# Down weights through two streams of buffers, and a new written order, in a one-core kernel of a long convolution with a routed FFN

## Chip, core and metric

One core of a Trainium2 chip. The metric is device microseconds of one launch, the median of three runs. A profiled execution is one more run, with the hardware profiler on; "span" is the time from its first to its last instruction.

## The reference

Inputs are q, k, v of 2048 x 512, float32. Cut to what matters:

```python
k_shift = sum over t in 0..3 of k_pad[:, t:t+S] * shift_k[:, 3-t]     # 4 taps, causal, per channel
kv = k_shift * v
y  = causal convolution of kv with ssm_k, 2048 long, per channel (by FFT) + kv * ssm_D
a  = q * y
r  = q @ w_r;  idx = the two tokens with the largest r
f  = (silu(x_sel @ w_gate) * (x_sel @ w_up)) @ w_down * sigmoid(r_sel)   # for these two tokens only
b  = q + f scattered to the two tokens
g  = sigmoid(q . gate_w)
out = g * a + (1 - g) * b
```

w_gate and w_up are 512 x 1792, w_down is 1792 x 512.

## The kernel before

The 512 channels are worked in four blocks c = 0..3 of 128. The long convolution is a transform of 2048 points, cut in two short stages with a 32 x 32 transpose between, done for kv and for the filter, a product, and the way back. For a block the steps are, with the name that they have in the written order:

- `D t` (L138): POOL adds the skip weight into the filter tile hN; one for each of the eight hN tiles, t = 2c and 2c + 1.
- `A c.b` (L152): first stage of the filter, two matmuls from hN, then a DVE transpose into tile e (L150).
- `taps c.x` (L163): the four taps. ScalarE scales (L168, L175), POOL adds (L177); in two of the sixteen groups DVE does both (L172).
- `T c.x` (L179): 16 TensorE transposes of the taps' result, then two DVE products with vN (L192).
- `C c.b` (L197): first stage of kv, as A.
- `S c.u` (L208): second stage, 16 matmuls; ScalarE copies one half (L222), DVE multiplies (L229), and every second S has two sums over tile y (L237) on POOL (on DVE for S3.6 and S3.7).
- `I c.u` (L240): back, first stage, 16 matmuls into two PSUM tiles, each emptied by ScalarE (L259) or DVE (L261) into tile f. I3.1's second one is emptied by DVE.
- `X c.i` (L263): DVE transpose of half of f (L268).
- `J c.m` (L289): back, second stage. For c < 3: 8 matmuls, ScalarE applies the gate (L317), POOL multiplies by qN (L320), SP stores (L323). For c = 3: 16 matmuls, a DVE product (L310), a sum on POOL, or on DVE for J3.3 (L312), and the store. `Q 3.m` (L281) prepares q for the last block on ScalarE, `Y x` (L271) loads it.

The routed FFN is one generator, of which each `G` in the order takes one step, 43 in all: G1 to G8 the router scores (one qT tile each, L353), G9 the gates, G10 to G14 the two largest scores by four TensorE transposes (L340) with DVE and POOL steps between, G15 the token numbers and the gather of their rows (L386, an indirect DMA from POOL), G16 and G17 the gathered rows (L401, L408), G18 to G25 the gate weights and G26 to G33 the up weights (one tile each, L425), G34 the transpose of the product, G35 to G42 the down weights (L443; wd0 to wd7 below, wd0 and wd1 being the two halves of the first row block), G43 the sum over blocks (L452) and the scaling (L454). `Z0` (L457) adds the two rows into the output by an indirect DMA; it follows every store and G43.

Loads: each stream (L73) is a list of DMAs into a ring of tiles. `Lh` loads the filter tiles hN (2 buffers), `Lk` the taps' input kT (2), `Lv` vN (3), `Lq` qN (4), and `Lw` the stream wff (2): 8 qT tiles, 8 gate, 8 up and 8 down tiles, 32 loads. `L0` to `L10` load constants, w2 (the second stage's matrix) in two halves `L4` and `L5`, vv (J's matrix) by `L10`. All loads and stores are issued by SP, in order; a load waits until its buffer's last reader is done, and whatever is behind it on SP waits too.

What sets the order is the text ORDER (L33): a list of 533 names. At each name the step's generator is advanced by one piece, and what it emits goes to the end of the queue of its engine:

```python
    with tc.manual_schedule():
        for name in ORDER.split():
            next(work[name], None)
```

So every engine works strictly in the order of this text. PSUM holds three tiles "p2" for A, T, C, S, I and J3, one "ps" for the other J, one "pf" for the FFN.

Of the kernel before, what the change touches and what calls it, by code (L numbers as in the profile page):

```python
# [594 lines left out]
```

## Time and profile before

| what | value |
|---|---|
| median of 3 runs | 169.28 us (167.88, 169.28, 171.59) |
| the profiled execution | 167.47 us, span 165.7 us |
| busy: TensorE, VectorE, ScalarE, GpSimd | 132.6, 117.1, 105.7, 116.3 us |
| mean granted TensorE clock | 0.943 |
| moved by DMA | 39.8 MB |

How to read the lines below: engines are PE (TensorE matmuls), PEld (its weight loads), DVE (VectorE), ACT (ScalarE), POOL (GpSimd), SP (SyncE; SPq is its queue). A timeline row is: start us, length us, engine, line, operation, output and inputs, count, and in brackets how long the engine had been idle before and what ended that. One float32 matmul of the source is two MATMUL records, so an S is x32, a J of c < 3 x16, a down step x8. In a row of groups stand the busy time, the mean ns of one, and the idle time ahead of them.

### The profile page before, as it was taken

What the parts mean: (1) busy time and instruction counts of PE and PEld (TensorE: products, weight loads), DVE (VectorE), ACT (ScalarE), POOL (GpSimd) and SP (SyncE); (2) the same over time, 40 slices, a digit from 0 to 9 for tenths busy, and PEclk for the clock granted to TensorE, in tenths of its full rate; (3) what the DMA queues carried; (4) which work ended last, traced back from release to release, by engine and by line L of the source; (5) the groups of instructions that cost most, each with busy time, mean ns of one, the idle gap of its engine ahead of it and who ended that gap; (6) DMA issues with size and microseconds to landing.
All of it is one profiled execution on the core that took longest, in us unless ns stands there. A gap on an engine that the chain in (4) does not pass through costs nothing.

```text
span 165.7 us, 5116 instructions
## 1 busy us (share of the span) xinstructions
PE 132.6 (80%) x2156; PEld 64.0 (39%) x2156; DVE 117.1 (71%) x120; ACT 105.7 (64%) x201; POOL 116.3 (70%) x109
## 2 busy tenths in 40 slices
PE   0079699898859889489999999999999898696270
PEld 0033245442313333263446545355445454274040
DVE  0649899999654796644999769999929987673400
ACT  4537578847756457324679959865499888966010
POOL 0079899999776996824999999558936974077303
PEclk9999999999996999965999999999999999999955
DMA  5999999979993008903685671907778877898820
GB/s 175 303 381 352 333 403 398 377 267 337 408 362 102 0 6 357 365 13 120 252 277 192 235 285 20 321 19 248 230 243 266 279 267 200 237 299 276 304 104 1
DMA packets 16420, 39.82 MB, mean 240 GB/s; under 512 B 2123, under 2 KB 2828, under 8 KB 16270
## 3 DMA queue, kind: packets, MB, share of 16 engines
q1 hardware_dynamic: 16334, 39.50, 68.4%
q8 instruction: 17, 0.28, 0.6%
q0 software_dynamic: 64, 0.01, 0.1%
q14 instruction: 5, 0.04, 0.1%
HBM read 35.30 MB, written 4.20 MB: 238 GB/s over the span
## 4 chain that ended last, share of the span: by engine, by line
PE 42%; DMA 36%; DVE 9%; ACT 4%; SPq 3%; issue 3%; POOL 1%; POOLq 1%; DVEq 0%
DMA wff<-in_wd_dram 10%; PE p L217 9%; DMA vN<-in_vN_dram 9%; PE p L204 7%; PE p L159 7%; PE p L251 5%; PE pf L425 4%; PE ps L304 4%; DMA wff<-in_qT_dram 4%; DMA wff<-in_wu_dram 4%; DVE e L150 4%; DMA pe<-in_qrow_dram,ti 3%; DMA out_dram<-e 3%; ACT f L259 3%; DMA w<-in_w_dram 3%; DVE y L229 3%
## 5 line engine op out<-in xcount | busy, mean ns | idle before, releaser
L177 POOL TENSOR_TENSOR acc<-acc,tap 128x512 f32<-128x512 f32 x42 | 53.6, 1284 | 7.0 <-ACT tap L175 5.7
L229 DVE TENSOR_TENSOR y<-p,g 128x1024 f32<-128x1024 f32 x32 | 38.0, 1214 | 13.7 <-ACT g L222 12.8
L150 DVE STREAM_TRANSPOSE e<-p 128x1024 f32<-128x1024 f32 x32 | 38.2, 1230 | 7.6 <-PE p L204 3.2
L237 POOL TENSOR_TENSOR y<-y 128x512 f32<-128x512 f32 x30 | 38.1, 1288 | 5.2 <-DVE fac L412 3.3
L175 ACT ACTIVATE tap<-kT,shk 128x512 f32<-128x512 f32 x42 | 29.7, 723 | 10.7 <-POOL acc L177 10.4
L217 PE MATMUL p<-e,w 64*32 64x256 f32 x1024 | 34.8, 393 | 1.2 <-DVE kv L192 0.6
L159 PE MATMUL p<-hN,w 64*128 64x512 f32 x64 | 20.3, 724 | 10.7 <-DMA w<-in_w_dram 9.4
L222 ACT ACTIVATE g<-p 128x512 f32<-128x512 f32 x32 | 18.8, 599 | 13.6 <-PE p L217 13.0
L217 PEld LDWEIGHTS p<-e,w 64*32 64x32 f32 x1024 | 16.7, 107 | 20.4 <-ACT f L259 3.5
L320 POOL TENSOR_TENSOR qN<-acc,qN 128x512 f32<-128x512 f32 x12 | 15.4, 1288 | 11.9 <-DMA qN<-in_qN_dram 11.3
L317 ACT ACTIVATE acc<-ps,omg,gcol 128x128 f32<-128x128 f32 x48 | 18.1, 461 | 6.6 <-PE ps L304 6.4
L204 PE MATMUL p<-kv,w 64*128 64x512 f32 x64 | 16.6, 640 | 3.3 <-ACT f L259 2.0
L259 ACT ACTIVATE f<-p 128x1024 f32<-128x1024 f32 x15 | 16.3, 1115 | 4.7 <-PE p L251 4.7
L268 DVE STREAM_TRANSPOSE f<-f 128x2048 f32<-128x2048 f32 x8 | 18.1, 2298 | 0.1
L251 PE MATMUL p<-y,w 32*64 32x512 f32 x256 | 16.9, 601 | 0.3 <-DVE e L150 0.3
L168 ACT ACTIVATE acc<-kT,shk 128x512 f32<-128x512 f32 x16 | 11.4, 720 | 4.7 <-DMA kT<-in_kT_dram 3.1
L304 PE MATMUL ps<-f,vv 128*64 128x128 f32 x192 | 13.3, 278 | 0.3 <-ACT acc L317 0.3
L304 PEld LDWEIGHTS ps<-f,vv 128*64 128x64 f32 x192 | 10.3, 134 | 5.9 <-issue 2.7
L159 PEld LDWEIGHTS p<-hN,w 64*128 64x128 f32 x64 | 5.9, 209 | 16.3 <-POOL hN L141 9.8
L192 DVE TENSOR_TENSOR kv<-p,vN 128x512 f32<-128x512 f32 x16 | 10.5, 686 | 1.3 <-DMA vN<-in_vN_dram 1.0
L443 PE MATMUL pf<-wff,pe 112*32 112x256 f32 x64 | 5.6, 422 | 6.8 <-DMA wff<-in_wd_dram 6.7
L204 PEld LDWEIGHTS p<-kv,w 64*128 64x128 f32 x64 | 6.1, 192 | 11.2 <-issue 7.6
(72 smaller groups left out, 99.6 us busy)
## 6 DMA issues: line engine op xcount, KB each, us to landing
vN<-in_vN_dram SPq DMA_DIRECT2D x16, 256.0 KB, 6.4
hN<-in_hN_dram SPq DMA_DIRECT2D x8, 512.0 KB, 5.6
wff<-in_qT_dram SPq DMA_DIRECT2D x8, 512.0 KB, 6.0
wff<-in_wg_dram SPq DMA_DIRECT2D x8, 448.0 KB, 3.7
wff<-in_wu_dram SPq DMA_DIRECT2D x8, 448.0 KB, 4.6
wff<-in_wd_dram SPq DMA_DIRECT2D x8, 448.0 KB, 5.3
qN<-in_qN_dram SPq DMA_DIRECT2D x12, 256.0 KB, 5.8
out_dram<-qN SPq DMA_DIRECT2D x12, 256.0 KB, 3.6
```

Of the source, the lines that this page charges most:

```text
L150: nc.vector.transpose(ee[c][:, i, b * 16:(b + 1) * 16].rearrange("p d k e -> p d e k"), p)
L159: nc.tensor.matmul(p[:, j], w1[r], hs.get(t)[r, 16 * (b % 2):16 * (b % 2) + 16], start=True, stop=True)
L175: nc.scalar.activation(s, w[j], AF.Copy, scale=shk[:, c, j:j + 1])
L177: nc.gpsimd.tensor_add(acc, acc, s)
L204: nc.tensor.matmul(p[:, par].rearrange("p (d e) m -> p d e m", e=2), w1[r], x[r], start=True, stop=True)
L217: nc.tensor.matmul(p[32 * j:32 * j + 32, b, ri].rearrange("p i d -> p (i d)"), w2[r, 4 * u + j, 32 * ri:32 * ri + 32], e[r, :, u + 8 * j, ...
L222: nc.scalar.activation(g, p[:, :, :, 0], AF.Copy)
L229: nc.vector.tensor_mul(y[:, u % 2], p[:, :, :, 1].unsqueeze(3).to_broadcast(shape), g.unsqueeze(2).to_broadcast(shape))
L237: eng.tensor_tensor(w[:, :, 0, n], w[:, :, 0, n], w[:, :, 1, 1 - n], op=op)
L251: nc.tensor.matmul(pp[kp // 2][64 * h:64 * h + 64, kp % 2], w3[r, n], y[(h - kp) % 2][r, :, 0, n], start=(n == 0), stop=(n == 1), skip_gro ...
L259: nc.scalar.activation(to, src, AF.Copy)
L304: nc.tensor.matmul(p[64 * par:64 * par + 64, w * i:w * i + w], vv[:, par * 16 + m0 + i, :], ff[c][:, d, par * 16 + m0 + i, :], start=(i == ...
```

## The change

The four second halves of the down weights (wd1, wd3, wd5, wd7) are no longer loaded by the stream wff but as tiles 8 to 11 of the filter stream hN, whose two buffers the filter's first stage uses until A3.3. wff has 28 loads instead of 32. The array of down weights is laid out as 32 x 32 blocks in its last two dimensions to fit the tile; the bytes and their order are the same, each load is 448 KB as before. With the two wff buffers, four down loads can be under way. The text ORDER is new throughout; it holds the same names, with 12 Lh and 28 Lw instead of 8 and 32.

```diff
--- before.py
+++ after.py
@@ -31,28 +31,28 @@
 
 
 ORDER = """
-Lk L0 taps0.0 taps0.0 Lk Lk Lv L3 Lh L7 L2 Lv L1 Lh Lk Lw Lw taps0.2 taps0.0 taps0.2 taps0.0 taps0.2 taps0.1 D0
-taps0.1 taps0.1 taps0.1 A0.1 A0.1 A0.0 T0.0 D1 A0.3 taps0.2 T0.0 T0.0 Lk Lh Lv Lk Lv taps0.3 taps0.3 taps0.3 taps0.3
-taps1.0 D2 taps1.0 taps1.0 taps1.1 taps1.0 taps1.1 taps1.1 A0.3 A0.0 G A0.2 A0.2 G T0.1 T0.1 T0.1 A1.1 Lk A1.1 Lw Lk
-Lw Lv L4 L5 Lv C0.0 C0.0 C0.1 C0.1 C0.2 C0.2 C0.3 C0.3 taps1.1 taps1.3 taps1.3 taps1.2 G G A1.0 A1.0 T1.0 T1.0 T1.0
-S0.3 S0.3 taps1.3 S0.3 S0.4 S0.4 taps1.2 taps1.3 S0.4 Lw S0.2 S0.2 S0.2 taps1.2 S0.0 S0.0 G Lv S0.0 Lw Lh Lv Lk
-taps1.2 S0.5 S0.5 S0.5 G T1.1 S0.1 S0.1 T1.1 T1.1 S0.1 taps2.0 D3 S0.3 S0.3 S0.5 taps2.0 S0.1 Lw Lk Lw L6 A1.2 C1.0
-A1.2 taps2.1 C1.0 A1.3 A1.3 G G L9 C1.2 G C1.2 C1.1 C1.1 G taps2.1 S0.1 S0.6 S0.6 taps2.0 G I0.0 Lk Lh Lq L10
-taps2.1 Lk Lv taps2.0 S0.6 G Lh D5 C1.3 C1.3 Lv taps2.1 G Lq I0.0 taps2.3 Lv Lk A2.3 S0.7 I0.0 taps2.3 A2.3 D4 S0.7
-S0.7 S1.2 S1.2 S1.2 S0.5 A2.1 A2.1 taps2.3 taps2.3 S1.3 S1.3 S1.3 T2.0 A2.2 S0.7 T2.0 T2.0 G A2.0 A2.0 A2.2 S0.7
-taps2.2 taps2.2 taps2.2 G I0.1 I0.1 I0.1 Lh S1.0 taps2.2 S1.5 S1.5 S1.5 S1.1 S1.0 S1.0 G S1.1 S1.1 Lw Lk T2.1 G Lv
-Lh G S1.4 S1.4 T2.1 T2.1 Lq Lw G Lv Lw Lw S1.4 Lk Lv C2.1 C2.1 C2.0 C2.0 C2.2 C2.2 C2.3 C2.3 G S1.3 X0.1 X0.0
-taps3.1 S1.3 S1.1 S1.1 G I1.0 taps3.1 Lw Lw taps3.1 taps3.1 taps3.0 taps3.0 S1.5 I1.0 I1.0 taps3.0 S1.5 taps3.0 S1.7
-S1.7 S1.7 D7 S1.6 S1.6 S1.6 S2.2 Lk D6 taps3.2 G G J0.3 J0.3 Lv taps3.2 S2.2 Lw Lw T3.0 S1.7 S1.7 T3.0 T3.0 taps3.2
-taps3.2 Lq A3.3 A3.3 J0.2 S2.2 J0.3 J0.2 J0.2 S2.3 S2.3 S2.3 G G I1.1 I1.1 S2.0 S2.0 S2.3 S2.0 S2.1 S2.1 J0.1 I1.1
-S2.1 A3.2 J0.1 Lv A3.2 Lw S2.3 Lw A3.1 taps3.3 J0.3 G G S2.1 A3.1 J0.0 Lw S2.1 X1.1 I2.0 taps3.3 J0.0 X1.0 I2.0 A3.0
-A3.0 I2.0 S2.7 S2.7 S2.7 taps3.3 G S2.6 S2.6 S2.6 S2.5 S2.5 S2.5 J0.2 Lq taps3.3 J0.1 Lw S2.4 S2.4 T3.1 T3.1 Y1 T3.1
-S2.4 S2.7 J1.0 J1.0 G S2.7 C3.0 C3.0 J1.0 Lw S2.5 S2.5 Lq J1.0 Lw Q3.2 C3.1 C3.1 C3.3 C3.3 C3.2 C3.2 J1.2 J1.2 I2.1
-I2.1 I2.1 S3.3 S3.3 S3.2 G G S3.3 S3.2 S3.2 Lq Q3.3 S3.1 S3.1 S3.0 S3.0 Q3.3 J0.0 J0.0 S3.1 S3.0 S3.5 S3.5 S3.5 Y0
-J1.1 Lw Lw X2.1 S3.4 J1.1 J0.1 J1.2 J1.2 S3.4 Q3.2 G G S3.4 J1.3 J1.3 Lq S3.3 S3.3 S3.1 S3.1 I3.0 I3.0 G Lw X2.0
-S3.6 S3.6 S3.6 S3.7 S3.7 S3.7 J2.1 J2.1 Lq G J1.1 J1.1 Lw G J1.3 J1.3 S3.5 S3.5 L8 S3.7 S3.7 I3.0 Lq Lw Lw J2.3 J2.3
-I3.1 I3.1 J2.2 G I3.1 Lq Lq J2.2 Q3.0 G J2.0 J2.0 J2.1 J2.1 Lw Lw J2.2 X3.0 J2.3 J2.0 Q3.1 Q3.0 J2.3 X3.1 J2.2 Q3.1
-J3.0 J3.1 G G J3.2 J3.1 J3.1 J3.3 J3.0 J3.0 J3.2 J3.2 J3.3 J3.3 J2.0 Lw Lw G G J3.1 G J3.0 J3.2 J3.3 Z0
+Lk L0 taps0.0 taps0.0 Lk Lk Lh Lk L2 L3 L7 Lh L1 Lv Lw Lv Lw taps0.1 taps0.0 taps0.1 taps0.0 taps0.2 taps0.2 D0
+taps0.2 taps0.1 taps0.1 A0.0 A0.0 A0.1 T0.0 D1 taps0.2 G taps0.3 taps0.3 taps0.3 T0.0 A0.1 A0.2 A0.2 T0.0 A0.3 A0.3
+G taps0.3 T0.1 Lk Lh Lv Lv Lw Lk Lh Lk Lk Lw L4 Lv taps1.0 D2 taps1.0 taps1.0 taps1.0 taps1.1 taps1.1 D3 taps1.1
+taps1.1 taps1.2 A1.0 T0.1 T0.1 A1.0 C0.2 C0.1 C0.2 C0.1 C0.0 G C0.0 C0.3 C0.3 A1.2 A1.2 A1.1 A1.3 G S0.0 A1.3 A1.1
+taps1.3 taps1.2 S0.0 taps1.3 S0.0 S0.3 T1.0 S0.3 S0.1 taps1.2 taps1.3 S0.1 T1.0 S0.3 Lw Lv L5 Lw Lk Lv taps1.2
+taps1.3 G Lv Lk S0.4 S0.4 T1.0 S0.1 S0.4 taps2.0 G T1.1 T1.1 T1.1 Lw Lw S0.1 S0.1 L6 S0.5 taps2.0 S0.5 S0.5 S0.2
+C1.3 S0.2 S0.2 Lk L9 taps2.1 C1.3 C1.1 C1.1 G G C1.2 C1.2 C1.0 Lk taps2.0 S0.3 S0.3 S0.5 C1.0 S0.5 G I0.0 taps2.0 Lq
+G G S0.6 I0.0 taps2.1 G S0.6 S0.6 taps2.2 S0.7 S0.7 S0.7 taps2.1 Lh D4 I0.0 taps2.2 G A2.1 A2.0 A2.1 G A2.0 S1.3
+S1.3 S1.3 S1.2 S1.2 S1.2 Lh S0.7 S0.7 taps2.2 taps2.1 I0.1 D5 G Lk taps2.3 A2.2 A2.2 I0.1 I0.1 S1.1 S1.1 S1.1 S1.0
+S1.0 S1.0 S1.4 S1.4 S1.4 S1.5 S1.5 Lv T2.0 T2.0 S1.5 taps2.3 taps2.2 G S1.3 S1.3 S1.1 S1.1 taps2.3 Lv Lk G T2.0 S1.6
+I1.0 S1.6 taps3.0 I1.0 L10 taps2.3 Lv Lw Lw taps3.0 I1.0 G G X0.1 X0.0 T2.1 J0.0 Lv T2.1 T2.1 S1.6 A2.3 A2.3 C2.3
+C2.3 C2.2 C2.0 C2.2 C2.1 C2.0 C2.1 taps3.0 taps3.1 S1.7 taps3.0 Lk Lh taps3.1 Lw taps3.1 Lv Lk Lw taps3.3 S1.7
+taps3.1 T3.0 G G J0.0 Lv S1.7 T3.0 S1.5 S1.5 taps3.3 T3.0 S1.7 S1.7 S2.1 S2.1 S2.1 Lv S2.0 S2.0 S2.0 S2.2 J0.3 I1.1
+J0.0 Lw Lw S2.2 Lq J0.0 Lh taps3.3 S2.2 J0.3 Lq J0.1 G taps3.3 I1.1 I1.1 G X1.1 S2.3 J0.1 S2.3 S2.3 S2.5 S2.5 S2.5
+D6 S2.4 S2.4 S2.4 J0.2 A3.1 A3.1 A3.0 S2.1 S2.1 Lw Lw taps3.2 L8 A3.0 J0.1 G S2.3 J0.2 S2.3 X1.0 taps3.2 taps3.2 Lq
+G I2.0 I2.0 D7 S2.6 J0.1 Lv S2.6 S2.6 Lq S2.7 S2.7 Lw Lw S2.7 J0.3 taps3.2 J1.0 S2.7 Y0 I2.0 T3.1 T3.1 S2.5 S2.5
+T3.1 A3.2 A3.2 Y1 J1.0 Q3.3 G J1.0 S2.7 Lh G A3.3 A3.3 C3.1 C3.1 C3.2 C3.0 C3.0 Q3.0 C3.3 C3.3 Q3.1 J1.1 Lw G Lq
+J1.1 I2.1 I2.1 J0.3 J1.0 Lw Lw J0.2 C3.2 S3.1 S3.1 S3.1 J1.1 S3.0 S3.0 I2.1 S3.0 Lq Lq X2.0 S3.1 J1.1 Lh J1.3 J1.3 G
+G Lw Lw S3.3 S3.3 S3.3 S3.2 S3.2 S3.2 Q3.3 S3.4 S3.4 J1.2 S3.4 S3.5 S3.5 S3.5 G X2.1 J1.2 J1.3 S3.1 J1.3 S3.3 J0.2
+Q3.0 S3.3 G S3.6 S3.6 Lw Lw Q3.2 J1.2 I3.0 Lq J1.2 S3.6 J2.3 J2.3 G S3.7 S3.7 S3.7 S3.5 S3.5 Lw Lq G S3.7 S3.7 J2.0
+I3.0 Lq Lq G G I3.1 J2.0 J2.0 I3.0 J2.1 I3.1 I3.1 J2.1 G G J2.2 J2.2 X3.0 J2.3 Lh Lw J2.0 Lw J2.1 Q3.1 J3.0 Q3.2
+J3.1 X3.1 J3.2 Lh J2.3 J2.1 J2.2 J3.0 J3.0 J2.2 J3.0 J3.3 J3.1 J3.1 J3.2 J3.2 J3.1 G G J3.3 J3.3 J3.2 J3.3 G G G Z0
 """
 
 
@@ -94,13 +94,14 @@
                 self.load()
             return self.tiles[k // len(self.cuts)]
 
-    hs = Stream("hN", [128, 32, N2], [a["hN"][t] for t in range(2 * NC)], P["h"])
+
+    hs = Stream("hN", [128, 32, N2], [a["hN"][t] for t in range(2 * NC)] + [a["wd"][fb, :, 1] for fb in range(4)], P["h"])
     kst = Stream("kT", [128, 1216], [a["kT"][c, x] for c in range(NC) for x in range(2)], P["k"], [(0, 704), (704, 1216)])
     vst = Stream("vN", [128, 4, DC], [a["vN"][c, x] for c in range(NC) for x in range(4)], P["v"])
     qst = Stream("qN", [128, 4, 128], [a["qN"][c, m] for c in range(NC - 1) for m in range(4)], P["q"])
     side_src = [a["qT"][c, hf] for c in range(4) for hf in range(2)]
     side_src += [a[nm][hf, kc] for nm in ("wg", "wu") for hf in range(2) for kc in range(4)]
-    side_src += [a["wd"][fb, :, hf] for fb in range(4) for hf in range(2)]
+    side_src += [a["wd"][fb, :, 0].rearrange("p a b -> p (a b)") for fb in range(4)]
     sst = Stream("wff", [128, 1024], side_src, P["wff"])
 
     shk = const.tile([128, NC, 4], F32, name="shk")
@@ -438,7 +439,7 @@
         for fb in range(4):
             for hf in range(2):
                 yield
-                wt = sst.get(24 + 2 * fb + hf)
+                wt = hs.get(8 + fb).rearrange("p a b -> p (a b)") if hf else sst.get(24 + fb)
                 for s4 in range(4):
                     nc.tensor.matmul(pd[32 * s4:32 * s4 + 32, hf * 256:(hf + 1) * 256], hT[:FS, s4, 32 * fb:32 * fb + 32],
                                      wt[:FS, s4 * 256:(s4 + 1) * 256], start=(fb == 0 and hf == 0), stop=(fb == 3),
@@ -569,7 +570,7 @@
     r["wrg"] = wrg
     for n, w in (("wg", B_w_gate), ("wu", B_w_up)):
         r[n] = w.reshape(4, 128, 4, 2, HB).transpose(3, 0, 1, 2, 4).reshape(2, 4, 128, 4 * HB)
-    r["wd"] = B_w_down.reshape(4, 4, FS, 2, 256).transpose(0, 2, 3, 1, 4).reshape(4, FS, 2, 1024)
+    r["wd"] = B_w_down.reshape(4, 4, FS, 2, 256).transpose(0, 2, 3, 1, 4).reshape(4, FS, 2, 32, 32)
     return {n: np.ascontiguousarray(x) for n, x in r.items()}
 
 
```

## Prediction

> **What bounds the kernel now.** I read the chain that ended last from its end backwards, then the timeline of TensorE and its neighbours after 139 us, then the busy time by stretches. The chain's last pieces (start us, us, what):
>
> ```profile
> 20.14 8.93 DMA vN<-in_vN_dram
> ...
> 64.91 5.76 DMA pe<-in_qrow_dram,ti
> ...
> 124.00 6.09 DMA wff<-in_wu_dram
> ...
> 132.63 5.21 DMA wff<-in_wd_dram
> ...
> 138.58 6.59 DMA wff<-in_wd_dram
> ...
> 145.92 4.96 DMA wff<-in_wd_dram
> ...
> 151.56 2.04 PE p L304 x64
> ...
> 154.35 0.93 DVE e L312
> ...
> 155.30 5.60 DMA out_dram<-e
> ```
>
> From 132.6 to 150.9 us the chain is almost nothing but loads of the down weights: four rounds through two wff buffers, each round begun only when TensorE has left the buffer. The timeline of the same stage shows what they hold up:
>
> ```profile
> 139.86 1.97 PE L251 MATMUL p<-y,w 32*64 32x512 f32 x32
> 141.76 1.10 PE L304 MATMUL ps<-f,vv 128*64 128x128 f32 x16
> 141.97 1.24 DVE L261 COPY f<-p 128x1024 f32<-128x1024 f32 x1 [2.21 <-PE p L251]
> 143.31 4.50 DVE L268 STREAM_TRANSPOSE f<-f 128x2048 f32<-128x2048 f32 x2
> 150.92 0.64 PE L443 MATMUL pf<-wff,pe 112*32 112x256 f32 x8 [1.59 <-DMA wff<-in_wd_dram]
> 151.49 2.08 PE L304 MATMUL p<-f,vv 128*64 128x64 f32 x64
> 157.62 1.08 PE L443 MATMUL pf<-wff,pe 112*32 112x256 f32 x8 [0.55 <-DMA wff<-in_wd_dram]
> ...
> 161.34 0.30 ACT L454 ACTIVATE pe<-pf,fac 16x64 f32<-16x64 f32 x1 [1.98 <-PE pf L452]
> 161.93 1.38 POOL L457 DMA_INDIRECT out_dram<-pe,oidx  x1 [7.21 <-ACT pe L454]
> ```
>
> The two X3 transposes are through at 147.81, yet the last two J3 products (L304, x64) start at 151.49, behind the fifth and sixth down weights in TensorE's order. The scatter waits for two branches that end within 0.8 us of each other: the last store (155.30 + 5.60 = 160.90) and the routed tokens' row (161.34 + 0.30 = 161.64). Shortening one alone would bring at most 0.8 us.
>
> The stretches (start:end, length, then busy us of PE, PEld, DVE, ACT, POOL; granted clock, DMA share, GB/s) show the rest:
>
> ```profile
> 40.40:60.70 20.30, 16.73 (x215) 6.42 (x215) 13.14 (x19) 12.45 (x21) 16.64 (x20) 0.92 0.52 200
> 45.60:49.70 4.10, 2.21 (x34) 0.70 (x33) 2.12 (x5) 2.24 (x4) 3.20 (x6) 1.00 0.95 364
> 49.70:53.90 4.20, 4.13 (x25) 1.38 (x33) 1.76 (x4) 2.79 (x5) 2.77 (x6) 0.66 0.33 101
> 66.30:70.40 4.10, 1.89 (x72) 1.07 (x56) 2.75 (x5) 1.59 (x3) 3.58 (x4) 1.00 0.95 367
> 70.40:74.60 4.20, 3.64 (x40) 2.67 (x40) 1.91 (x5) 1.22 (x4) 0.89 (x2) 0.64 0.04 13
> 74.60:78.70 4.10, 4.10 (x48) 1.55 (x46) 1.80 (x2) 1.99 (x4) 2.02 (x3) 0.54 0.36 122
> 80.00:139.80 59.80, 57.58 (x1100) 28.77 (x1096) 52.14 (x44) 47.61 (x95) 47.15 (x40) 1.00 0.66 222
> 143.80:161.00 17.20, 10.09 (x200) 7.20 (x200) 7.70 (x7) 7.44 (x23) 7.62 (x6) 0.88 0.78 262
> ```
>
> From 80 to 139.8 us TensorE is busy 57.6 of 59.8 us: nothing is to be had there by order alone. Before it lie two holes. Around 66 to 70 us TensorE waits for the gathered rows, and its clock then stands at 0.64 and 0.54 for 8.3 us while all others are under half busy. Around 45 to 50 us it waits for the top-2 steps.
>
> **The change, part by part.** The instructions are the same; what changes is where eight loads land and the order. I compared the two ORDER lists name by name, with one unit price for each name from these rows (the L340 rows are tr1 to tr3, the first three of the four transposes in G11 to G14):
>
> ```profile
> 40.45 0.64 PE L353 MATMUL pf<-wff,wrg 128*32 128x256 f32 x8 [0.72 <-DMA wff<-in_qT_dram]
> 45.36 0.30 PE L340 MATMUL pf<-ident,m 128*128 128x128 f32 x1 [0.46 <-DVE m L337]
> 47.49 0.32 PE L340 MATMUL pf<-ident,m 128*128 128x128 f32 x1
> 50.86 0.32 PE L340 MATMUL pf<-ident,m 128*128 128x128 f32 x1
> 59.68 1.13 PE L159 MATMUL p<-hN,w 64*128 64x512 f32 x4 [0.43 <-DVE e L150]
> 70.71 1.17 PE L401 MATMUL pf<-wtrev,pe 2*128 2x32 f32 x8 [2.52 <-DMA pe<-in_qrow_dram,ti]
> 127.89 1.10 PE L217 MATMUL p<-e,w 64*32 64x256 f32 x32
> 130.13 0.59 PE L425 MATMUL pf<-wff,pe 128*32 128x224 f32 x8 [0.62 <-DMA wff<-in_wu_dram]
> 137.88 0.16 PEld L443 LDWEIGHTS pf<-wff,pe 112*32 112x32 f32 x8 [0.63 <-DMA wff<-in_wd_dram]
> L150 DVE STREAM_TRANSPOSE e<-p 128x1024 f32<-128x1024 f32 x32 | 38.2, 1230 | 7.6 <-PE p L204 3.2
> L177 POOL TENSOR_TENSOR acc<-acc,tap 128x512 f32<-128x512 f32 x42 | 53.6, 1284 | 7.0 <-ACT tap L175 5.7
> L188 PE MATMUL p<-ident,acc 64*128 64x64 f32 x128 | 6.5, 245 | 0.7 <-POOL acc L177 0.3 <-DVE y L229 0.3
> L192 DVE TENSOR_TENSOR kv<-p,vN 128x512 f32<-128x512 f32 x16 | 10.5, 686 | 1.3 <-DMA vN<-in_vN_dram 1.0
> ```
>
> So on TensorE an S costs 1.10, an A or C 1.13, an I 1.97, a T 0.81 (6.5 for eight), a J 1.10, two J3 2.08, a gate or up step 0.59, a down step 0.64.
>
> *Until the eighth qT step: 0.* G8 (old 40.45 us) has 12,521 KB of loads issued up to its own last one in both orders, and DMA is the busiest there. In between w2b comes 1,280 KB later and hN3 3,936 KB earlier; D3 now stands in POOL's queue ahead of two taps sums, so a late hN3 would hold POOL, but POOL also has two sums fewer ahead of G8 (2 × 1.28), which covers it. Without that cover it could cost as much, 2.6 us.
>
> *The gather: −2.5 and −3.4 us.* Ahead of G15 the new order has no longer two exchanges and the two products of T2.0 on DVE (2 × 1.23 + 2 × 0.69 = 3.8 us) nor the three sums of taps2.3 on POOL (3 × 1.28 = 3.8 us); TensorE's work ahead of G16, which uses the rows, stays the same (A2.3 leaves, S1.4 comes). The gather starts up to 3.8 us earlier against a wait of 2.52: the wait goes. Between gather and G16 lie A2.2, four S and T2.0, 6.3 us against 5.76 of transfer. Without the wait the half-clock stretch should go too: (1 − 0.64) × 4.2 + (1 − 0.54) × 4.1 = 3.4 us, in full, as no other engine was the limit. Bounds for both together: 0 (the wait forms again earlier) and −5.9, which I take.
>
> The Trainium skill, "TensorE: Matmul & The Clock Gate", Part 1, has the clock halved only after an idle window of about 3.4 us. The row says otherwise: a stretch of 4.1 us with 1.89 busy and no wait above 2.52 was enough. By the skill's rule the 3.4 us would have had another cause and might stay, and the sum would be 3.4 us higher.
>
> *New waits in the top-2 steps: +1.0 us.* Between tr1 and tr2, tr2 and tr3, tr3 and tr4 TensorE now has only S0.6 (1.10), S0.7 (1.10), and A2.1 with A2.0 (2.26). A step takes 2.13 us (45.36 to 47.49, nothing in its way) to 3.37 us (47.49 to 50.86, behind other DVE work); each carries its own 0.3. So the three waits are 1.4 to 4.7 us. Ahead of tr1 now stands I0.0, which needs POOL's sums of S0.3; POOL late by one sum makes it 1.3 more. Together 1.4 to 6.0, against 20.30 − 16.73 = 3.6 in the old stretch: −2.2 to +2.4. I take +1.0, in the upper half, because two sums of S0.5 and one of taps2.0 now stand in POOL's queue ahead of tr1's comparison.
>
> *G16 to G17: +0.5 us.* T2.1 stood between them and hid ScalarE's copy of the gathered rows; now nothing does. Nothing at best; at worst 1.2, as long as G16's own products (the 70.71 row).
>
> *Up weights: +0.7 us.* These loads share two buffers as before, and each pair waits for two gate or up steps. What TensorE has to do meanwhile is: before G26 7.2 us, before G28 6.8, before G29 5.3, before G31 5.5, before G33 (S3.6, I3.0, J2.3, and G32) 4.8. The old slowest up load took 6.09, the second of a pair; the first I put 0.8 us earlier (an estimate: their issues lie 0.4 apart and they share the queue). Then G30 waits 0.2, and G33, whose load is issued alone and 0.4 late, 1.7: together 1.9, less the old 0.62 and 0.63 of the rows above. Bounds: −1.2 (all hidden) and +2.2 (the second of a pair at 6.6, as the slowest down load: 0.7, 0.5 and 2.2).
>
> *The end: −4.3 us.* Ahead of I3.1 both orders have the same TensorE work (J2.0 and J2.1 change places), so with T its start, all after it can be laid side by side. Old T is 139.86. The copy, then X3.0 and X3.1, end at T + 7.95. New: no down weight stands between X3.1 and J3.2, J3.3; these start at T + 8.05, and by the old rows the last add ends 3.79 later (151.49 to 155.28) and the store 5.62 after that: T + 17.5. The other branch: wd1 and wd3 were issued around G27 and G29, wd0 and wd2 after G32 and G33, so G35 to G38 find them there. wd5 and wd4 need G36 and G35, wd6 and wd7 need G37 and G38 (done by T + 4.4); at the slowest 6.59 they land by T + 11.0. TensorE takes them after J3.3, T + 10.1, until T + 12.7, and copy, sum and scaling add 2.94 (157.62 + 1.08 to 161.64): T + 15.6. The later is T + 17.5 against 161.64 − 139.86 = T + 21.8. After G36, four loads and eight stores are 3.84 MB; at the 262 GB/s of the last row that is 14.7 us, inside 17.5. All of it leaves by SP's one queue, and wd6 and wd7 stand behind the store J2.0, which waits for POOL's product: that wait may eat up to 6 us before G41 is late.
>
> Sum on the profiled execution: 165.7 − 5.9 + 1.0 + 0.5 + 0.7 − 4.3 = 157.7 us of span. That execution took 167.47 us, 1.8 beyond its span, and the median of the three runs is another 1.8 above it: 161.3 us against 169.28.
>
> **The rivals.**
> - *The hole only moves.* The three top-2 steps and the gather are one chain; packed tighter, TensorE waits there what it waited at 70 us, and the half clock comes with it. For it: the 45.6 to 49.7 stretch was already half idle and paid 0.66 of clock. Against: the 3.8 us of DVE and POOL work are really gone from ahead of the gather. 165.7 + 2.2 − 4.3 = 163.6, so 167.2 us.
> - *The end stays bound by transfers.* The store J2.0 or the queue delays wd7 to beyond T + 17, and nothing of the 4.3 remains: the change then doesn't do what it says, there are not four loads in flight. For it: POOL had waited long for qN (below). Against: qN2.2 and 2.3 are now issued before G35. 165.7 − 5.9 + 2.2 = 162.0, so 165.6 us.
>
> ```profile
> POOL qN L320 <- DMA qN<-in_qN_dram: 11.3, 4, 4.9
> ```
> - *Late up weights, slower than before.* TensorE comes to G26 to G33 earlier, the loads don't. With a pair landing at 8.2 us (vN took 8.93 when DMA was full, so it can happen) the waits at the five places are 1.0, 1.4, 2.3, 2.1 and 3.8, together 10.6, less the old 1.2, and a half-clock stretch of 3.4 follows: 165.7 − 5.9 + 1.5 + 9.4 + 3.4 − 4.3 = 169.8, so 173.4 us. From about 7.4 us of landing on the kernel is slower than it was; below 7 it can't be. Against it: DMA is busy only 0.66 of the stretch up to 139.8. By the Trainium skill's idle window, cited above, only the last of these waits would lower the clock.
> - *No new wait at all:* 155.5, so 159.1 us.
>
> **How the numbers follow.** Forecast 161.3 us, 0.50; hole moves 0.17; end bound 0.14, about half of which lies beyond the 2% line; late loads 0.09; no new wait 0.10. A measurement of this kernel tells about 2% from no change: below 165.9 is faster, above 172.7 slower. Faster: 0.50 + 0.10 + 0.07, less 0.02 for the forecast's own tail, 0.65; slower 0.10, the late loads with a little of the hole; within 2% the rest, 0.25. Low end: no new wait, 159.1, less the 1.4 by which the lowest run lies under the median, 157.7. High end: the hole's 167.2 with the up loads at their bound (+1.5): 168.7.
>
> **What would show it.** Right: the wait at L401 is under 0.5 us and no stretch at 0.6 follows it; I3.1 starts near 136; no wait for wd over 0.5 us after X3; the scatter is released by the store of e, not by L454. Wrong: waits at L340 adding to over 4 us with a clock of 0.6 behind them; waits at L425 for wu over 2 us each; wd6 or wd7 landing after J3.3; or TensorE's idle time growing between 75 and 135 us, where I assumed the old density of 96%.

## The result, and the profile after

The changed kernel takes 156.87 us (median of four runs, 156.74 to 157.33); the kernel before, measured beside it, 170.3 us (167.88 to 171.59). The ratio is 0.9311, with a 95% interval of [0.9237, 0.9384]: faster, as forecast, and by more than forecast. The time lies 0.8 us below the low end of the predicted range. Its profiled execution took 156.97 us, of which the span is 155.2 us; before it was 167.47 and 165.7. Some executions of both kernels lie 1.6 to 5% above the fastest of their series, most of them at a lower clock; the ratios here leave them out, and a kernel with too few others has none. Lines of the new code are one higher than before (L341 was L340), and two higher where a run below adds a stream.

From the page of the changed kernel, the busy time of TensorE and the clock granted to it in 40 slices of the span:

```profile
PE 126.7 (82%) x2156; PEld 63.6 (41%) x2156; DVE 117.8 (76%) x120; ACT 105.6 (68%) x201; POOL 116.6 (75%) x109
PEclk9999999999999999999999999999999999999985
```

The same 2156 matmuls took 132.6 us before. The clock is now at 0.9 or more in every slice but the last two. What TensorE still waits for (us in all, times, longest):

```profile
PE pf L444 <- issue: 1.3, 1, 1.3
PE pf L426 <- DMA wff<-in_wu_dram: 1.3, 2, 0.8
...
PE pf L341 <- DVE m L338: 1.0, 2, 0.8
```

The wait for the gathered rows (L402) is no longer in the list, and L444, a down step, stands idle once, for 1.3 us; the profile names no releaser, and the step that follows is wd6's. The stretches (start:end, length, busy us of PE, PEld, DVE, ACT, POOL, granted clock, DMA share, GB/s), cut around the same stages as in the prediction:

```profile
9.40:42.90 33.50, 29.60 (x376) 12.69 (x376) 29.30 (x30) 20.26 (x32) 28.27 (x26) 1.00 0.95 336
42.90:60.00 17.10, 14.77 (x220) 5.54 (x216) 12.66 (x22) 12.43 (x21) 16.19 (x19) 1.00 0.56 203
60.00:71.40 11.40, 10.32 (x236) 5.51 (x232) 9.48 (x12) 8.55 (x16) 10.65 (x11) 1.00 0.49 176
71.40:80.00 8.60, 7.74 (x88) 3.83 (x92) 8.60 (x9) 7.52 (x11) 8.23 (x7) 1.00 0.82 284
80.00:133.20 53.20, 51.47 (x1013) 27.15 (x997) 44.33 (x38) 42.13 (x94) 41.06 (x35) 1.00 0.80 257
133.20:155.20 22.00, 12.78 (x260) 8.87 (x256) 10.64 (x10) 9.31 (x23) 10.63 (x8) 0.88 0.66 211
```

Neither the top-2 stage nor the gather's stage shows a clock under 1.00 any more, and the gather's wait is gone. Single instructions of the timeline, in the order of their start:

```profile
11.14 2.08 PE L160 MATMUL p<-hN,w 64*128 64x512 f32 x4 [11.14 <-POOL hN L142]
...
49.54 0.32 PE L341 MATMUL pf<-ident,m 128*128 128x128 f32 x1 [0.77 <-DVE m L338]
51.12 0.32 PE L341 MATMUL pf<-ident,m 128*128 128x128 f32 x1 [0.23 <-DVE m L338]
66.60 1.07 PE L402 MATMUL pf<-wtrev,pe 2*128 2x32 f32 x8
68.04 0.44 PE L409 MATMUL pf<-wrg,pe 128*32 128x32 f32 x8 [0.37 <-ACT pe L405]
133.20 2.17 PE L252 MATMUL p<-y,w 32*64 32x512 f32 x32
139.19 4.28 PE L305 MATMUL p<-f,vv 128*64 128x64 f32 x128
142.84 4.20 POOL L313 TENSOR_TENSOR e<-e 128x512 f32<-128x512 f32 x3
146.23 0.78 PE L444 MATMUL pf<-hN,pe 112*32 112x256 f32 x8
148.86 0.30 ACT L455 ACTIVATE pe<-pf,fac 16x64 f32<-16x64 f32 x1 [1.16 <-PE pf L453]
151.44 1.38 POOL L458 DMA_INDIRECT out_dram<-pe,oidx  x1 [4.40 <-DMA out_dram<-e]
```

I3.1 starts at 133.20 instead of 139.86 us, the four J3 products now run as one block of 4.28 us behind X3, and the scatter is released by a store of e, no longer by the scaled row. The last pieces of the chain (start us, us, what) tell what holds that store:

```profile
136.51 1.52 ACT acc L318 x4
...
139.29 1.51 ACT acc L318 x4
140.79 2.05 ACT e L289 x7
142.84 4.21 POOL e L313 x3
...
147.49 3.11 DMA out_dram<-e
```

No load of a weight is left in it. ScalarE's last work on J2 and q comes first, then three sums in a row on POOL, then one store.

### The profile page after: what moved, and what is told of

It is laid out like the page before. It is cut to its first block, busy times and chain, and to the rows that moved or that the text cites. A ratio compares the mean times of both kernels' runs of the same rounds, so it can differ in the third digit from the quotient of the medians.

```text
span 155.2 us, 5118 instructions
## 1 busy us (share of the span) xinstructions
PE 126.7 (82%) x2156; PEld 63.6 (41%) x2156; DVE 117.8 (76%) x120; ACT 105.6 (68%) x201; POOL 116.6 (75%) x109
## 4 chain that ended last, share of the span: by engine, by line
PE 36%; POOL 25%; DMA 13%; issue 7%; ACT 7%; DVE 6%; SPq 2%; POOLq 1%; ACTq 0%
POOL acc L178 15%; PE p L218 9%; PE ps L305 7%; PE p L252 7%; POOL y L238 6%; PE p L205 5%; DMA drow<-in_drow_dram 4%; DMA wff<-in_wu_dram 4%; PE pf L426 4%; PE p L160 3%; DVE f L269 3%; DVE y L230 3%; POOL e L313 3%; DMA hN<-in_hN_dram 3%; ACT f L260 2%
## 5 line engine op out<-in xcount | busy, mean ns | idle before, releaser
L218 PE MATMUL p<-e,w 64*32 64x256 f32 x1024 | 33.0, 379 | 1.4 <-ACT f L260 0.7
L160 PE MATMUL p<-hN,w 64*128 64x512 f32 x64 | 18.7, 693 | 12.3 <-POOL hN L142 12.3
L252 PE MATMUL p<-y,w 32*64 32x512 f32 x256 | 17.5, 600 | 0.3 <-DVE e L151 0.3
L205 PE MATMUL p<-kv,w 64*128 64x512 f32 x64 | 16.0, 624 | 1.4 <-DVE kv L193 1.2
L173 DVE SCALAR_TENSOR_TENSOR acc<-kT,shk,acc 128x512 f32<-128x512 f32 x6 | 5.0, 827 | 6.6 <-ACT acc L169 6.5
```

The lines of the kernel that those rows point to most:

```text
L160: nc.tensor.matmul(p[:, j], w1[r], hs.get(t)[r, 16 * (b % 2):16 * (b % 2) + 16], start=True, stop=True)
L205: nc.tensor.matmul(p[:, par].rearrange("p (d e) m -> p d e m", e=2), w1[r], x[r], start=True, stop=True)
L218: nc.tensor.matmul(p[32 * j:32 * j + 32, b, ri].rearrange("p i d -> p (i d)"), w2[r, 4 * u + j, 32 * ri:32 * ri + 32], e[r, :, u + 8 * j, ...
L252: nc.tensor.matmul(pp[kp // 2][64 * h:64 * h + 64, kp % 2], w3[r, n], y[(h - kp) % 2][r, :, 0, n], start=(n == 0), stop=(n == 1), skip_gro ...
```

## The experiments

My theory: the end is the later of two branches, and the change shortens both. The **row branch** runs from the last up weight (G33) over the eight down steps to the scaled row, the **convolution branch** from I3.1 over X3 and J3 to the last store of e. The new order brings the convolution branch forward, the four buffers the row branch. The rival: the gain is the order's alone (the holes at 50 and 70 us), and the buffers hardly matter. The table holds what the runs below gave: the time is the median of a kernel's runs, the rest is from its one profiled execution; G33, I3.1 and G42 (the last down step) are starts on TensorE in us.

| kernel | time | before, beside it | G33 | I3.1 | G42 | scatter, released by |
|---|---|---|---|---|---|---|
| before | 170.3 | | 130.13 | 139.86 | 157.62 | 161.93, row |
| new order, two buffers | 165.22 | 167.87 | 129.59 | 136.53 | 155.80 | 160.18, row |
| new head, old tail, two buffers | 164.83 | 167.87 | 129.34 | 138.91 | 156.01 | 160.54, row |
| old order, four buffers (first) | 170.96 | 167.87 | 134.65 | 145.92 | 158.60 | 165.29, store |
| old order, four buffers (b) | 167.94 | 169.82 | 129.16 | 140.06 | 153.89 | 161.98, store |
| old head, new tail, four buffers | 173.09 | 167.87 | 134.85 | 148.72 | 163.75 | 168.82, store |
| new order, three rounds | 162.93 | 169.82 | 128.77 | 132.94 | 152.39 | 156.76, row |
| changed | 156.87 | 170.3 | 129.03 | 133.20 | 146.23 | 151.44, store |

**The order alone: new_order_two_buffers.** The code of before (all eight down loads through wff) with the new order; each down load stands right behind the step that frees its buffer (against the changed kernel's order; the places from which its Lh and Lw for down weights are taken out aren't shown):

```diff
-J2.3 J2.3 G S3.7
+J2.3 J2.3 G Lw S3.7
...
-I3.0 Lq Lq G G I3.1
+I3.0 Lq Lq G Lw G Lw I3.1
...
-J2.1 G G J2.2
+J2.1 G Lw G Lw J2.2
...
-J3.1 G G J3.3
+J3.1 G Lw G Lw J3.3
```

> The new order with all eight down weights through the two wff buffers, as the old kernel loads them, each load at the earliest place that two buffers allow. My theory (the gain is made in two places that add, 6.7 us before I3.1 by the order and 3.8 us after it because the down weights lie ready): the stretch up to I3.1 stays as it is (start of I3.1 near 133 us), and after it the seventh and eighth down weights are issued only after G39 and G40, land about 17.5 us after the start of I3.1 and hold the end for about 4.1 us: 161 us instead of 156.9. Rival (the order alone makes the gain, the buffers add nothing): 157 us, within 0.5 of the changed kernel.

Measured: 165.22 us, 0.9832 [0.9768, 0.9896], so a gain, but one of about 2% at most. Its timeline, at the second down step, at the last pair of them and at the scatter:

```profile
135.96 0.64 PE L443 MATMUL pf<-wff,pe 112*32 112x256 f32 x8 [2.57 <-DMA wff<-in_wd_dram]
...
154.82 2.06 PE L443 MATMUL pf<-wff,pe 112*32 112x256 f32 x16 [6.77 <-DMA wff<-in_wd_dram]
160.18 1.38 POOL L457 DMA_INDIRECT out_dram<-pe,oidx  x1 [10.20 <-ACT pe L454]
```

Without the 2.57 us I3.1 would have started at 133.96, close to the changed kernel's 133.20: the order does bring the convolution forward. But the row branch still goes through four rounds of two loads, from G33 to G42 26.2 us (27.5 before, 17.2 in the changed kernel), and the scatter waits for it. Of 5.9 us that the order is worth there, 1.8 are left at the scatter. The rival expected 157, I expected 161: both too low.

**The buffers alone: old_order_four_buffers and its variant b.** The code of the changed kernel with the old order, down loads as early as the buffers allow; in the first, wd1 and wd3 stand between and behind the last up loads, in b behind wd0:

```diff
# first
-J1.1 Lw Lw X2.1
+J1.1 Lw Lh Lw Lh X2.1
# b
-I3.0 G Lw X2.0
+I3.0 G Lw Lh Lh X2.0
# both
-Lw G J1.3
+Lw G Lw Lh J1.3
...
-I3.0 Lq Lw Lw J2.3
+I3.0 Lq J2.3
...
-Q3.0 G J2.0
+Q3.0 G Lw Lh J2.0
...
-J2.1 J2.1 Lw Lw J2.2
+J2.1 J2.1 J2.2
...
-J2.0 Lw Lw G G
+J2.0 G G
```

> The old order with only the down weights' streams changed and their loads put as early as the four buffers allow. My theory: the stretch up to I3.1 stays (its start near 139.9 us), the waits for wd vanish, J3.2 starts near 149.3 instead of 151.5, and the release of the scatter comes 2 to 3 us earlier: 2.9 us less than before. Rival (order alone): no change, within 0.5 us of before. Rival (the buffers are the whole gain): 10 us less than before.

> The old order with four buffers again, but wd1 and wd3 are issued with wd0, after G34, where they no longer stand between the last two up loads. Theory (two branches that end together: the FFN's, whose last eight loads go in rounds of two buffers, and the convolution's, which has 5 us more of its TensorE work left at G33 in the old order; the later one is the end): the waits for wd vanish, J3 starts about 2 us earlier, and the convolution's branch keeps the end: 1 to 3 us less than before. Rival (the two edits simply add, the buffers being worth what the new order loses without them, some 8 us): 8 us less.

Measured: the first 171.05, 170.88, 173.0 and 166.22 us, before beside it 167.87, no ratio. These runs show no gain, and lie too far apart to rule out a small one. One of TensorE's waits in its trace, which is that of the run of 171.05 us:

```profile
PE pf L426 <- DMA wff<-in_wu_dram: 2.8, 1, 2.8
```

The last up step was late. Its load was issued at 126.81 us, between the down loads of 126.27 and 127.22, and took 7.79 us. The old head with the new tail below has the same loads in this order and a wait of 3.1 us at this place; variant b, which has them behind wd0, has no such wait. In the changed kernel a down load also goes out ahead of two up loads, but 2.2 us ahead (115.35 and 117.53), and the waits there are 0.8 and 0.5 us. Variant b took 167.94 us (165.3 to 168.58), before beside it 169.82, no ratio: 1.9 us less by the medians, 3.0 by the lowest runs, and no more can be said of its size. Its scaled row and its scatter:

```profile
157.17 0.31 ACT L455 ACTIVATE pe<-pf,fac 16x64 f32<-16x64 f32 x1 [1.98 <-PE pf L453]
...
161.98 1.38 POOL L458 DMA_INDIRECT out_dram<-pe,oidx  x1 [3.90 <-DMA out_dram<-e]
```

This is the clearest row of the study. The row is ready 4.2 us earlier than before (157.48 against 161.64), and the scatter starts at 161.98 instead of 161.93, because the last store of e now releases it. In this execution, shortening one of two branches that end together brought nothing, where the prediction's first part allowed 0.8 us at most.

**Half of the order: new_head_old_tail and old_head_new_tail.** The first takes the new order up to I3.1 and the old one behind it, with two buffers; the second the old order with four buffers up to I3.1 and the new one behind it. No diff is shown: each is one half of one list and what is then left of the other, in its sequence.

> The new order up to I3.1, then what is left in the old order's sequence, all down weights through the two wff buffers. My theory: 6.7 us less than before (start of I3.1 near 133 us and from there about 25.8 us to the end, as before). Rival (what the head saves was only there because the down loads had left wff): the head saves under 3 us.

> The old order up to I3.1, then what is left in the new order's sequence, with four buffers. My theory: 3.8 us less than before (start of I3.1 near 139.9, from there 22 us to the end). Rival (head and tail depend on each other, the tail can only be short when the loads of qN and the stores are early, as in the new head): under 2 us less than before.

Measured: 164.83 us, 0.9848 [0.9811, 0.9885], where I expected 6.7 us less than before, and 173.09 us, 1.0335 [1.0287, 1.0383], where I expected 3.8 us less: the second is slower than before. Four rows of TensorE and POOL of the first:

```profile
136.00 1.08 PE L443 MATMUL pf<-wff,pe 112*32 112x256 f32 x8 [2.86 <-DMA wff<-in_wd_dram]
...
146.18 2.09 PE L304 MATMUL p<-f,vv 128*64 128x64 f32 x64 [1.84 <-DVE f L268]
...
154.81 0.64 PE L443 MATMUL pf<-wff,pe 112*32 112x256 f32 x8 [3.09 <-DMA wff<-in_wd_dram]
...
160.54 1.38 POOL L457 DMA_INDIRECT out_dram<-pe,oidx  x1 [7.67 <-ACT pe L454]
```

Most of the head's gain is spent before I3.1, which starts at 138.91: 2.86 us of wait for wd1, then low clock (0.64 from 138.9 to 143.0 us), with J2.1's product, which stands ahead of I3.1 here, at 1.98 us instead of 1.10. The waits of the second from 120 us on:

```profile
PE pf L426 <- DMA wff<-in_wu_dram: 3.4, 2, 3.1
PE ps L305 <- ACT acc L318: 3.2, 3, 1.7
PE p L305 <- DVE f L269: 2.2, 1, 2.2
```

Behind the old head, with wd1 and wd3 between the up loads as in the first kernel above, TensorE waits for an up weight, then for ScalarE and VectorE. From I3.1 to the scatter it takes 20.1 us, 2.0 less than before, but I3.1 comes 8.9 us later than before. My expectation of 3.8 us less, a plain carry-over of the end term, fell here: that term isn't a property of the tail alone. How much of the loss is the up load's and how much the tail's isn't separated: the new tail with the loads placed as in variant b was not run.

**One round more: new_order_three_rounds.** In the changed kernel only wd1 and wd3 go through hN (the lines that give wd5 and wd7 to wff are left out):

```diff
-    hs = Stream("hN", [128, 32, N2], [a["hN"][t] for t in range(2 * NC)] + [a["wd"][fb, :, 1] for fb in range(4)], P["h"])
+    hs = Stream("hN", [128, 32, N2], [a["hN"][t] for t in range(2 * NC)] + [a["wd"][fb, :, 1] for fb in range(2)], P["h"])
...
-J2.3 Lh Lw J2.0
+J2.3 Lw J2.0
...
-J3.2 Lh J2.3
+J3.2 J2.3
...
-J3.1 G G J3.3
+J3.1 G Lw G Lw J3.3
```

> The new order with only wd1 and wd3 through hN; wd0, wd2 and wd4 to wd7 share the two wff buffers, so from the last up step (G33) on there are three rounds of loads where the changed kernel has two and the kernel before has four. Theory (the FFN's branch is paced by rounds of 5 to 7 us): between the changed kernel and the new order with two buffers, from G33 to G42 about 22 us (17.2 and 26.2 there), total about 160.5 us. Rival (what matters is that the first two rounds are ready when TensorE comes, at I3.1): like the changed kernel, within 1 us.

Measured: 162.93 us, 0.9645 [0.9566, 0.9723], 2.4 us above what I expected; G33 to G42 23.6 us (22 expected), and:

```profile
151.29 2.18 PE L444 MATMUL pf<-wff,pe 112*32 112x256 f32 x16 [7.10 <-DMA wff<-in_wd_dram]
...
156.76 1.38 POOL L458 DMA_INDIRECT out_dram<-pe,oidx  x1 [10.73 <-ACT pe L455]
```

With the head unchanged (I3.1 at 132.94), one more round at the end costs 6.1 us of time. Once the convolution is out of the way, fewer rounds of loads mean less time, though not in equal shares: 165.22, 162.93, 156.87 us for four, three and two rounds (I3.1 is 3.3 us later in the first of these, 0.3 earlier in the second).

**The gather's wait put back: new_order_early_px.** In the changed kernel G16, which uses the gathered rows, stands three S and T2.0 ahead of where it was:

```diff
-S1.1 S1.1 S1.1 S1.0
+S1.1 S1.1 S1.1 G S1.0
...
-taps2.3 taps2.2 G S1.3
+taps2.3 taps2.2 S1.3
```

> The changed kernel with one step moved: G16 stands ahead of S1.0, so TensorE comes to the gathered rows some 4 us earlier than it did and waits for them about 2.4 us, as the kernel before did. Theory (such a wait costs itself, and the half-clock stretch that followed it in the kernel before is a consequence of it): a stretch of clock near 0.6 after it, start of I3.1 and the end later by 2.4 to 5.8 us. Rival one (the wait costs itself but not the clock): 2.4 us. Rival two (DVE and POOL set the pace of this stage, TensorE catches up): under 1 us.

Measured: 163.44 us (161.39 to 166.52), no ratio; its profiled execution 162.11 us, 5.1 more than that of the changed kernel. G16 on TensorE, then the stretches around it:

```profile
64.87 1.91 PE L402 MATMUL pf<-wtrev,pe 2*128 2x32 f32 x8 [2.54 <-DMA pe<-in_qrow_dram,ti]
```

```profile
60.00:64.90 4.90, 1.86 (x37) 0.52 (x33) 2.85 (x5) 2.73 (x4) 4.25 (x6) 0.96 0.62 245
64.90:72.30 7.40, 7.40 (x120) 4.69 (x120) 2.42 (x2) 1.85 (x4) 3.24 (x4) 0.56 0.01 2
```

A wait of 2.54 us brought 7.4 us at 0.56 of the clock: (1 − 0.56) × 7.4 = 3.3 us more, 5.8 in all. G18 starts 5.7 us later than in the changed kernel, I3.1 5.9. So the prediction's −2.5 and −3.4 are one thing, and in this kernel the second follows from the first.

**The late start: new_order_drow_first.** The changed kernel's first matmul starts at 11.14 us, 1.7 later than before: POOL's first step on hN waits for drow, whose load now stands behind the first filter tile. Put back ahead of it:

```diff
-Lk L0 taps0.0 taps0.0 Lk Lk Lh Lk L2 L3 L7
+Lk L0 taps0.0 taps0.0 Lk Lk L3 Lh Lk L2 L7
```

> The changed kernel with the load of drow (65 KB) issued ahead of hN0. The first TensorE instruction waits for the skip of hN0 until 11.1 us there, and that for drow, which lands at 10.7. Theory (the start is lost time): first TensorE work near 9.6 us, and the whole 1.5 us earlier. Rival (up to G8 the loads set the pace, so an earlier first step only waits later): the same time within 0.4 us.

Measured: 156.1 us (155.68 to 157.28), 0.9228 [0.9153, 0.9303]; the changed kernel had 156.87 and, in a second measurement below, 156.47. A gain of 0.4 to 0.8 us, less than these runs can separate. TensorE's first row, three at the end, and the scatter:

```profile
10.36 3.58 PE L160 MATMUL p<-hN,w 64*128 64x512 f32 x8 [10.36 <-DMA w<-in_w_dram]
...
145.81 0.38 PE L444 MATMUL pf<-hN,pe 112*32 112x256 f32 x1 [2.52 <-issue]
...
147.98 1.89 PE L453 MATMUL pf<-pe,sel 128*16 128x64 f32 x16 [0.75 <-ACT pe L448]
150.49 1.38 POOL L458 DMA_INDIRECT out_dram<-pe,oidx  x1 [5.33 <-ACT pe L455]
```

I3.1 came 1.2 us earlier, the last store landed at 149.01 instead of 150.60 us, and the scatter started 0.95 us earlier. The rest went to the row branch, which now releases it: L444 stands idle for 2.52 us instead of 1.31, the clock falls (0.61 from 145.8 to 150.0 us), and the sum over blocks takes 1.89 us instead of 1.07.

**What bounds the end now: new_order_split_sums, new_order_six_buffers, all_three, beside changed_again.** The first moves one of POOL's three J3 sums to VectorE and two of ScalarE's steps on q forward; the second loads wd5 and wd7 early into the kT buffers, free by then; the third does both, and takes drow first:

```diff
# split sums
-JADD = "GGGV"
+JADD = "GVGV"
...
-J2.1 G G J2.2 J2.2 X3.0 J2.3 Lh Lw J2.0 Lw J2.1 Q3.1 J3.0 Q3.2 J3.1
+J2.1 G G J2.2 Q3.1 J2.2 Q3.2 X3.0 J2.3 Lh Lw J2.0 Lw J2.1 J3.0 J3.1
...
-J3.3 J3.1 J3.1 J3.2 J3.2 J3.1 G
+J3.3 J3.1 J3.2 J3.2 J3.1 J3.1 G
# six buffers (Lm loads a stream of its own, wd5 and wd7 into tiles kT)
-G X2.1 J1.2
+G X2.1 Lm J1.2
...
-Lw Lw Q3.2 J1.2
+Lw Lw Q3.2 Lm J1.2
...
-J2.3 Lh Lw J2.0
+J2.3 Lw J2.0
...
-J3.2 Lh J2.3
+J3.2 J2.3
```

> The changed kernel itself, as the measure for the three beside it. Both theories: 156.9 us, within 0.5 us, span 155.2; G8 at 42.4, I3.1 at 133.2, G42 at 146.2, the scatter at 151.4, released by the store of e.

> The changed kernel with the sum of J3.1 moved from POOL to VectorE and the second steps of Q3.1 and Q3.2 put around the ACT step of J2.2. Theory: the last store is bound by POOL's three J3 sums (142.84 to 147.05); with two of them POOL ends at about 145.7, and VectorE, which takes the fourth after its last product, at about 145.8. The last store then lands at about 149.3, where the scaled row is ready at 149.16: so 1 to 1.5 us less, and the scatter is released by the two branches within 0.5 us of each other. Rival (the end is bound by the transfers of the stores, not by the sums): within 0.4 us of the changed kernel.

> The changed kernel with wd5 and wd7 loaded at 118 to 126 us into the buffers of kT, free by then, so six down loads are in flight and two are left for the end. Theory of two branches: the row branch gets 1.3 to 2 us shorter (G42 at about 144.5 instead of 146.23, no wait over 0.5 at L444), but the last store stays at about 150.6, so the time is within 0.5 us of the changed kernel; at best 0.7 us come back through a less crowded queue for the qN rows and the stores. Rival (each buffer more is worth its share, as from two to three to four rounds less: 165.2, 162.9, 156.9): 2 us or more less.

> L3 ahead of the first Lh, two sums on VectorE with the earlier second steps of Q3.1 and Q3.2, and six down loads in flight. Theory of two branches: both get shorter, so the gains come back together: drow 1.2 us (I3.1 at about 132.0), the end T+16 instead of T+18.2 to the scatter; 2.3 to 3 us less than the changed kernel, about 154. Rival (a plain sum of the three single results): what drow alone gave (0.8 us) plus what the other two give alone in these runs.

Measured: changed_again 156.47 us, 0.9328 [0.9234, 0.9422]; new_order_split_sums 156.72, 0.9352 [0.9249, 0.9454]; new_order_six_buffers 157.1, 0.9382 [0.9294, 0.9471]; all_three 156.71, 0.9342 [0.9261, 0.9424]. Nothing separates them. The last piece of the chain with the sums split:

```profile
145.61 4.44 DMA out_dram<-e
```

The last sum was done 1.5 us earlier (145.59 against 147.05), and the last store took 4.44 us instead of 3.11, so the scatter came only 0.6 us earlier. The four stores were issued closer together (143.4 to 145.6 us, against 144.2 to 147.5), as the rival would have it, but that this made the last one long isn't shown: in all_three, with the same split, they were issued from 145.7 to 148.0 us, and the last one took 3.32 us. With six buffers the waits for up weights:

```profile
PE pf L427 <- DMA wff<-in_wu_dram: 3.5, 3, 1.4
```

The changed kernel had 1.3 us of such waits, and 1.5 when it was run again. Of the three waits here, the first (0.9 us) comes before any of the early loads is issued; the other two, 1.4 and 1.2 us, are for up loads issued 0.9 and 0.4 us ahead of the first early load. That sharing with it made them late is my reading, not shown. The tail got shorter, from I3.1 to the scatter 17.1 us instead of 18.2, but I3.1 came later (137.16 in its profiled execution, the longest of its six). In all_three the tail is 16.6 us, I3.1 at 135.47; the first of these rows belongs to its start, the second to the up weights:

```profile
22.54 4.45 PE L206 MATMUL p<-kv,w 64*128 64x512 f32 x12 [2.50 <-DVE kv L194]
```

```profile
PE pf L427 <- DMA wff<-in_wu_dram: 2.3, 3, 1.5
```

Up to there the order is that of new_order_drow_first, where the same step waited 0.60 us and took 2.95; here a product on VectorE that had itself waited 1.56 us for vN, and the low clock behind it, cost 2.8 us by G8 (43.63 against 40.80). My expectation of 154 us fell: the tail gained 1.6 us, and the head lost more.

That low clock at C0 (the first stage of kv for the first block, the row above) doesn't need a long wait. Two more executions, with the same steps and nearly the same waits of TensorE ahead (0.95 and 0.60 us in new_order_two_buffers, 0.88 and 0.61 in new_order_early_px), differ in it. The stretch from 22.5 to 27.0 us, of the first and of the second:

```profile
22.50:27.00 4.50, 4.50 (x18) 1.81 (x18) 3.05 (x3) 2.82 (x5) 3.99 (x5) 0.63 1.04 411
22.50:27.00 4.50, 4.50 (x26) 1.89 (x28) 4.31 (x4) 2.80 (x6) 4.06 (x5) 1.00 1.03 411
```

The same step takes 4.57 us in the first and 2.95 in the second, and G8 follows at 43.5 and 42.1 us.

## Why the prediction was right, and where it was wrong

The direction and the main mechanism held: four loads in flight and no wait for the gather. The size was too small by 2.5 us of span (157.7 forecast, 155.2 measured), and by 1.9 us in what was added to it: I carried over that the median lay 1.8 us above the profiled execution, and after the change it lies 0.1 below (156.87 against 156.97). That 1.8 was scatter between runs of the kernel before. The time landed under the range because these errors add.

| term of the sum | forecast | measured | from |
|---|---|---|---|
| until G8 | 0 | +1.95 | 40.45 to 42.40 |
| wait for the gather | −2.5 | −2.5 | no wait at L402 |
| half clock behind it | −3.4 | −3.4 | clock 1.00 from 60 to 80 us |
| half clock at 49.7 to 53.9 | not counted | −1.4 | (1 − 0.66) × 4.2 |
| top-2 waits | +1.0 | −1.2 | TensorE's idle time in the stretch: 3.57 to 17.10 − 14.77 = 2.33 |
| G16 to G17 | +0.5 | +0.4 | 0.37 |
| up weights | +0.7 | 0.0 | 1.3 against 0.62 + 0.63 |
| the rest up to I3.1 | | −0.5 | remainder |
| I3.1's start | −3.7 | −6.7 | 139.86 to 133.20 |
| from there to the end | −4.3 | −3.8 | 25.84 to 22.0 |

*Until G8.* The step failed: I compared the bytes issued up to G8 and not which load the first matmul needs. POOL's fewer sums, named there as the cover for a late hN, do not cover a wait for drow; that the price without that cover, 2.6 us, is near is chance, as it was worked out for another load. With drow ahead G8 came at 40.80, against 42.0 to 42.8 in six executions with drow behind; where the clock fell at C0 it came at 43.5 to 43.7, whichever load was first.

*The gather.* Right in both terms, and new_order_early_px shows it in reverse. The Trainium skill's "TensorE: Matmul & The Clock Gate", Part 1, which asks for an idle window of about 3.4 us, does not agree: a stretch of 4.9 us with 1.86 busy and no wait above 2.54 was enough. The Trainium skill has that window, in the same part, run freely and not start with the kernel. If so, the place of a gap in it could count, which would fit that like waits end in different clocks here; no run tests it.

*The top-2 steps.* The mis-sized term, and a misread row. I set new waits at the top-2 steps against all of TensorE's idle time in the old stretch, 3.6 us, but at L340 it had waited only 0.46 us there. Its longest wait was for something else, a copy out of PSUM by ScalarE:

```profile
49.77 1.16 PE L204 MATMUL p<-kv,w 64*128 64x512 f32 x4 [1.96 <-ACT f L259]
```

The new order has no such wait. Its waits at L341 are 0.77 and 0.23 us, with 0.92 more for POOL's step on hN (L142) ahead of A2.1, so the top-2 steps did cost TensorE more than before; the stretch as a whole still lost 1.2 us of idle time. My upper bound for a step, 3.37 us, held 0.9 us in which tr3 stood behind that late matmul and 1.1 behind other VectorE work; in the new order tr1 to tr2 takes 2.12 (47.42 to 49.54) and tr2 to tr3 1.58 (49.54 to 51.12). I chose the upper half of the range for POOL's queue, and no wait at tr1 came of it. And the 0.66 of clock behind the 1.96 us is gone too; it stood in my own quoted row, and the sum left it in.

*Up weights.* Two waits, 0.77 and 0.52 us, where I had 0.2 and 1.7: within the bounds, but at G31 and G32 and not at G30 and G33. And of the old waits that I took off, the 0.63 is one for a down weight (L443), not for an up weight.

*The end.* Near in sum, by two errors that cancel. The last sum ends at 147.05, T + 13.9, where I had T + 11.8: I took the old distance from J3's products and overlooked that three sums follow each other on POOL, behind J2's products. The last store took 3.11 us where I had 5.62 from a row under load. So it lands at T + 17.4 against a forecast T + 17.5, and the row is ready at T + 16.0 against T + 15.6. The scatter is released by the store, as forecast. The half microsecond between −4.3 and −3.8 lies behind that landing: 4.6 us to the end of the span, 4.06 from the row to the end before.

*The signs.* Of the signs of being right, two came out otherwise: I3.1 started at 133.2 and not near 136, and L444 stood idle 1.31 us after X3. That idle time ends at 145.77, behind J3.3's products (143.47), so wd6 very likely landed after them: one of the signs of being wrong. It cost nothing, because the row was ready 1.4 us before the store landed.

*The sum as a sum.* It was right only because both branches got shorter together. By the ratios order alone gave 1.7% and both gave 6.9%; buffers alone (b) have no ratio. By the start of the scatter, against 161.93 us before, order alone gave 1.75 us, buffers alone nothing, and both 10.5 us. By the sum's terms the order alone would have been worth 3.7 and the buffers alone up to 4.3: too much for each, and too little for the two.

*The rivals.* "The hole only moves" is refuted by the stretches: clock 1.00 and no wait over 0.92 us at the top-2 steps. "The end stays bound by transfers" is what happens with four or three rounds of loads, not with two. "Late up weights" did not come here, but did in the old head with the new tail, which was slower than before, and, milder, with six buffers: that rival's place was right, and in the old head the wait came where a down load was issued right ahead of the last up load. "No new wait" was the nearest, 159.1 us, or 157.7 at its lowest run.

What stays open: why the clock falls at C0 in some executions and not in others, which makes about 1.5 us at G8; why the first matmul of the new order starts anywhere from 10.5 to 11.8 us; and what made the last store of new_order_split_sums long. None of these was tried by itself.

## What to carry to other kernels

Where two branches end together, price an edit by the branch that ends later after it, and expect edits on the two to be worth little singly and more together, as here. A wait on TensorE of about 2.5 us can cost more than twice its length (5.8 us for 2.54 here), though one of 2.57 cost no clock; and where a stretch of low clock stood behind a wait, it went when the wait went. A load moved earlier on one queue can make the loads behind it late: name the step that waits for those before counting the gain. And an idle stretch is to be taken apart by what each wait in it was for, before it is put down to one cause.
